# Sliding-window attention and top-1 experts on one core: a chunk's two score halves made next to each other, its second exponentials ahead of the other chunk's transposes' copy, and logits and row sums handled for several chunks at once

## The chip, the cores and the metric

One core of one Trainium2 chip runs the whole program in one launch. The metric is the device time of one execution in microseconds (us); the time before is the median of three runs, 646.98 us (646.08 to 647.4).

## The reference, cut to what matters

```
B, H, S, D = 8, 8, 576, 64            # attention
scores = q @ k.T / sqrt(D) + slope[h] * -(i - j)   where 0 <= i - j < 128, else -1e9
p = exp(scores - rowmax);  attn = p / (p.sum(-1) + 1e-9);  x = attn @ v    -> (4608, 512)
E, F = 8, 1024                        # experts, one for each token
logits = x @ w_gate;  e = argmax(logits);  gate = softmax(logits)[e]
out = gate * (relu(x @ w1[e]) @ w2[e])
```

Everything is float32. The expert part first needs to know which tokens go to which expert, and so the whole attention.

## The kernel before, in words

The 4608 tokens are worked on in 36 **chunks** of 128 query rows. Nine chunks make up two sequences: four of the first sequence (block m = 0, 1, 2, 3), one **tail chunk** with the last 64 rows of both, four of the second sequence. For m = 0 there is only one block of keys, otherwise two. A chunk passes through these stages; the line numbers are those of the profile of before.

- **Score half** `g` = 0 or 1 (four heads each; `scores`, L167 and L176): TensorE writes the bias (bfloat16 products with `eye_sb`) and then the products of `q_sb` and `k_sb` into one of two PSUM tiles, `s0` and `s1`, which take turns. All of these matmuls use 64 x 64 quarters of the array, four at a time. The first half of a chunk is in `s0`, the second in `s1`.
- **Weigh** (`weigh`): VectorE folds the band with a predicated copy (L189, not for m = 0) and takes the row maximum `nmax` (L192); ScalarE makes four exponentials (L198) into `pe`, each followed by a read of its accumulator, the row sum `rsum`. These free the score tile.
- **Transposes** of a half (`transposes`, L211): four 128 x 128 transposes on TensorE into a bank of PSUM (`b_ps`, two buffers), ScalarE copies it to `pT` (L213), GpSimd masks it with two selects (L221, L223).
- **Value products** (`av`, L239): `pT` times `v_sb`, 128 x 64 of the array, into another `b_ps`. They are short for a chunk with m = 0. ScalarE copies the result to `xT` (L286).
- **Rows** (`rows`): VectorE takes the reciprocal of `rsum` (L246); TensorE multiplies `xT` with the identity and the gate weights (L249, "logit products" below) into the single tile `r_ps`; VectorE scales both parts (L254) into `x_sb`, sums the logits over heads (`done`, L1220), and SyncE's queue writes the rows to `xd` in DRAM (L1227). GpSimd adds 1e-9 to `rsum` (`guard`, L182).

The order on every engine is written by hand: time is cut into **steps**, four for each chunk, and `LAGS` says at which step after 4 x chunk each stage k stands: 0 and 4 are the score halves, 2 and 5 their maxima and exponentials, 1 and 6 the transposes, 7 and 8 the value products, 3 the rows, 9 the copy to `xT`; `rank` sorts within a step. So TensorE always has stages of several chunks in a row: scores of chunk c beside transposes of c-1, value products of c-2 and logit products of c-3 or c-4. Every engine runs its list in order and waits on semaphores.

After a group of 3 to 6 chunks (`GROUPS`) `route` ranks the group's tokens by expert, in five stages spread over steps, most of them at every fourth step: mostly small VectorE operations, two bursts of small matmuls (L490 to L494, and L537). Steps also carry DMA loads (`load_q`, `load_v`, `load_k`, expert weights `w_raw`), GpSimd's scaling of `q_sb` (L70), and from step `FETCH` on the rounding of the first expert weights, half a matrix at a time, on ScalarE (L1011) and GpSimd (L1016).

Around step 144 the first expert's early tokens are gathered (`e_xg`); they go through TensorE transposes (L672, at two steps, "p0" and "p1"), a ScalarE cast `e_xh` (L674) and the first layer (L711) between the last chunks. From about 217 us TensorE does the layers of the experts (L711, L907) to the end.

Of the kernel before, what the change touches and what calls it, by code (L numbers as in the profile page):

```python
# [21 lines left out]
QB = 32  # L22
# [13 lines left out]
def attention(ctx, tc, st, qT, kT, v, iw, load_c2, chunk_done, chunks, begun):  # L36
# [75 lines left out]
    eps_sb = const.tile([128, H], F32, name="eps_sb")  # L112
# [68 lines left out]
    def guard(rsum):  # L181
        nc.gpsimd.tensor_tensor(out=rsum, in0=rsum, in1=eps_sb, op=ALU.add)  # L182

    def weigh(g, pe, rsum, s_ps, m, tail, lo, hi, later=False, add=True):
# [9 lines left out]
        def exps(pairs=range(2)):  # L194
            for n in pairs:
# [6 lines left out]
            if add and g and 1 in pairs:  # L202
                guard(rsum)
# [39 lines left out]

    def rows(ch, subs, xT, rsum):
        rinv = small.tile([128, H], F32, name="rinv")
        nc.vector.reciprocal(out=rinv, in_=rsum)  # L246
# [3 lines left out]
        x_sb = xp.tile([128, NP, XW], F32, name="x_sb")  # L250
        for lo, n in ((128, E), (0, D)):
            cols = slice(lo, lo + 2 * n)
            split = lambda ap: ap[:, :, cols].rearrange("q p (c x) -> q p c x", c=2)
            nc.vector.tensor_tensor(  # L254
                out=split(x_sb), in0=split(r_ps),
# [19 lines left out]
    for ch in range(len(chunks)):  # L275
# [4 lines left out]
        if ch in SPLIT:  # L280
            plan.setdefault(4 * ch + 3, []).append((10, ch))
# [6 lines left out]
    def do(k, ch):  # L288
        if k == 9:
            return copy_x(ch)  # L290
        if k > 10:
            h = slice(4 * k - 44, 4 * k - 40)
            nc.vector.tensor_reduce(out=sums[ch][:, h], in_=pes[ch][:, h, :], axis=AX.X, op=ALU.add)
            return guard(sums[ch]) if k == 12 else None
        if k == 10:
            exps = second.pop(ch)
            exps((0,))
            copy_x(ch - 2)
            return exps((1,))
        subs = chunks[ch]  # L300
        if k in (0, 4):
            if k == 0:
                pes[ch] = pp.tile([128, H, 128], F32, name="pe")
                sums[ch] = small.tile([128, H], F32, name="rsum", bufs=8)
            live[ch] = scores(subs, k // 4)
        elif k in (2, 5):
            second[ch] = weigh(k // 3, pes[ch], sums[ch], *live.pop(ch), later=k == 5 and ch in SPLIT, add=ch not in SUMS)
# [3 lines left out]
        elif k == 3:  # L311
            rows(ch, subs, xTs.pop(ch), sums.pop(ch))
# [981 lines left out]
```

## Time and profile before

| what | value |
|---|---|
| median of 3 runs | 646.98 us (646.08 to 647.4) |
| profiled execution, its own time | 646.91 us |
| span from its first to its last instruction | 645.2 us |
| TensorE (PE) matmul busy | 632.1 us, 98% |
| VectorE (DVE), ScalarE (ACT), GpSimd (POOL) busy | 390.9, 314.1, 299.2 us |
| granted TensorE clock, mean | 0.998 |

The profile gives each instruction's engine, line, output and inputs, start and duration; times are from the span's start. "Idle" notes in brackets name what ended a wait. Matmuls are pipelined: one that is listed with 0.32 us is followed by the next after much less, so the price of a stage is read from start to start. ScalarE's and VectorE's operations overlap their neighbours a little in the same way. PEld is TensorE's loading of weights.

### The profile page before, as it was taken

What the parts mean: (1) busy time and instruction counts of PE and PEld (TensorE: products, weight loads), DVE (VectorE), ACT (ScalarE), POOL (GpSimd) and SP (SyncE); (2) the same over time, 40 slices, a digit from 0 to 9 for tenths busy, and PEclk for the clock granted to TensorE, in tenths of its full rate; (3) what the DMA queues carried; (4) which work ended last, traced back from release to release, by engine and by line L of the source; (5) the groups of instructions that cost most, each with busy time, mean ns of one, the idle gap of its engine ahead of it and who ended that gap; (6) DMA issues with size and microseconds to landing.
All of it is one profiled execution on the core that took longest, in us unless ns stands there. A gap on an engine that the chain in (4) does not pass through costs nothing.

```text
span 645.2 us, 15063 instructions
## 1 busy us (share of the span) xinstructions
PE 632.1 (98%) x5681; PEld 540.2 (84%) x5681; DVE 390.9 (61%) x978; ACT 314.1 (49%) x947; POOL 299.2 (46%) x414
## 2 busy tenths in 40 slices
PE   8999999999998999999999999999999999999995
PEld 4888888888887988888988898898898888888884
DVE  6578888969898785545544654555455355346411
ACT  5878889888867324433333334334233333424311
POOL 5534657769446040166236707633660660561202
PEclk9999999999999999999999999999999999999999
DMA  9958998988734263372534325333442542534101
GB/s 312 301 153 216 220 260 237 217 258 240 193 69 103 54 196 98 130 273 75 186 128 151 108 78 183 113 94 139 142 122 83 165 122 87 185 107 143 65 0 62
DMA packets 57645, 97.90 MB, mean 152 GB/s; under 512 B 11669, under 2 KB 31765, under 8 KB 56674
## 3 DMA queue, kind: packets, MB, share of 16 engines
q1 hardware_dynamic: 49090, 76.89, 39.9%
q0 software_dynamic: 8336, 19.76, 10.6%
q8 instruction: 46, 0.75, 0.5%
q10 hardware_dynamic: 144, 0.26, 0.2%
q14 instruction: 29, 0.24, 0.1%
HBM read 77.91 MB, written 18.98 MB: 150 GB/s over the span
## 4 chain that ended last, share of the span: by engine, by line
PE 67%; ACT 0%; DVE 0%; issue 0%; POOLq 0%; POOL 0%; ACTq 0%
PE y_ps L907 32%; PE l_ps L711 30%; PE s_ps L711 2%; PE x_ps L672 1%; PE b_ps L239 1%; PE y_ps L867 1%; PE r_ps L249 0%; PE x_ps L867 0%; ACT pe L198 0%; POOLq L1060 0%; PE l_ps L683 0%; DVE y L915 0%; DVE nmax L192 0%; ACT e_xh L674 0%; DVE s_ps L189 0%
## 5 line engine op out<-in xcount | busy, mean ns | idle before, releaser
L714 ACT ACTIVATE hh<-l_ps 128x336 fp32r<-128x336 f32 (+7 forms) x104 | 45.9, 446 | 203.4 <-PE l_ps L711 176.9
L718 DVE SCALAR_TENSOR_TENSOR hl<-l_ps,hh 128x336 fp32r<-128x336 f32 (+7 forms) x104 | 51.7, 501 | 152.4 <-ACT hh L714 137.5
L691 POOL DMA_INDIRECT xg<-xd,od_idx x112 | 114.8, 1025 | 35.1 <-issue 34.8
L198 ACT ACTIVATE pe<-s_ps,nmax 128x128 f32<-128x128 f32 x288 | 102.9, 382 | 33.7 <-DVE nmax L192 27.0
L907 PE MATMUL y_ps<-wh,hh 128*128 128x512 f32 (+5 forms) x280 | 111.0, 397 | 0.0
L907 PE MATMUL y_ps<-wh,hl 128*128 128x512 f32 (+5 forms) x280 | 110.4, 394 | 0.0
L907 PE MATMUL y_ps<-wl,hh 128*128 128x512 f32 (+5 forms) x280 | 110.3, 394 | 0.0
L895 POOL DMA_INDIRECT out<-y,od_pidx x33 | 34.6, 1049 | 147.8 <-ACT y L913 141.2
L999 DVE TENSOR_TENSOR wl<-w_raw,wh 128x512 fp32r<-128x512 f32 x114 | 73.9, 690 | 32.0 <-ACT wh L995 27.4
L711 PE MATMUL l_ps<-xh,wh 128*128 128x304 f32 (+9 forms) x416 | 81.8, 318 | 0.3 <-DVE hl L718 0.3
L711 PE MATMUL l_ps<-xl,wh 128*128 128x304 f32 (+9 forms) x416 | 81.1, 316 | 0.3 <-issue 0.3
L711 PE MATMUL l_ps<-xh,wl 128*128 128x304 f32 (+9 forms) x416 | 81.0, 317 | 0.0
L711 PEld LDWEIGHTS l_ps<-xh,wh 128*128 128x128 f32 x416 | 68.0, 189 | 9.0 <-issue 1.2
L711 PEld LDWEIGHTS l_ps<-xl,wh 128*128 128x128 f32 x416 | 66.3, 189 | 2.3 <-issue 0.6
L711 PEld LDWEIGHTS l_ps<-xh,wl 128*128 128x128 f32 x416 | 66.4, 189 | 1.9
L239 PE MATMUL b_ps<-pT,v_sb 128*64 128x128 f32 (+2 forms) x1136 | 65.4, 265 | 0.4 <-ACT pT L213 0.4
L239 PEld LDWEIGHTS b_ps<-pT,v_sb 128*64 128x64 f32 (+1 forms) x1136 | 56.1, 136 | 10.0 <-issue 4.9
L907 PEld LDWEIGHTS y_ps<-wh,hl 128*128 128x128 f32 (+5 forms) x280 | 51.4, 184 | 13.7 <-DVE hl L718 0.2
L907 PEld LDWEIGHTS y_ps<-wl,hh 128*128 128x128 f32 (+5 forms) x280 | 51.5, 184 | 11.3
L907 PEld LDWEIGHTS y_ps<-wh,hh 128*128 128x128 f32 (+5 forms) x280 | 51.4, 184 | 10.4 <-ACT hh L714 0.5
L995 ACT CAST wh<-w_raw 128x1024 fp32r<-128x1024 f32 x57 | 59.5, 1044 | 1.0 <-DMA w_raw<-w 1.0
L198 ACT ACTIVATION_READ_ACCUMULATOR pe<-s_ps,nmax 128x1 f32 x272 | 59.6, 219 | 0.0
(225 smaller groups left out, 958.2 us busy)
## 6 DMA issues: line engine op xcount, KB each, us to landing
w_raw<-w SPq DMA_DIRECT2D x64, 512.0 KB
q_sb<-qT SPq DMA_DIRECT2D x39, 256.0 KB
xd<-x_sb SPq DMA_DIRECT2D x32, 258.0 KB
v_sb<-v SPq DMA_DIRECT2D x32, 256.0 KB
k_sb<-kT SPq DMA_DIRECT2D x7, 1152.0 KB
w_n<-w SPq DMA_DIRECT2D x4, 1024.0 KB
xg<-xd,od_idx POOLq DMA_INDIRECT x112
xd<-x_sb SPq DMA_DIRECT2D x8, 129.0 KB
```

Of the source, the lines that this page charges most:

```text
L198: nc.scalar.activation(out=pe[:, h, :], in_=s_ps[:, c, n, lo:lo + 128], func=AF.Exp, bias=nmax[:, 2 * c + n:2 * c + n + 1], scale=1.0, **( ...
L239: nc.tensor.matmul(out=x_ps[64 * c:64 * c + 64, p, q], lhsT=blocks["v", b, m - 1 + kb][0:kk, D * h:D * h + D], rhs=pT[0:kk, kb, h, q], sta ...
L672: nc.tensor.transpose(out=x_ps[:, d, :], in_=g[:, SUB * d:SUB * d + 128], identity=st["ident"])
L691: ins = tc.nc.gpsimd.indirect_dma_start(out=g[:, s], out_offset=None, in_=parts, in_offset=bass.IndirectOffsetOnAxis(ap=idx[:, s], axis=0),)
L711: nc.tensor.matmul(out=ps, lhsT=a[:, 128 * d:128 * d + 128], rhs=b[:, d], start=(k == 0), stop=(k == 11))
L714: nc.scalar.activation(out=hh, in_=ps, func=AF.Relu)
L718: nc.vector.scalar_tensor_tensor(out=hl, in0=ps, scalar=0.0, in1=hh.bitcast(F32), op0=ALU.max, op1=ALU.subtract)
L867: nc.tensor.matmul(out=ps[m * g:m * g + n], lhsT=hrs[p][:, f, :], rhs=w2s[p][:, f % 4, w * g:w * g + w], start=f == 0, stop=f == 7)
L895: ins = nc.gpsimd.indirect_dma_start(**kw).ins
L907: nc.tensor.matmul(out=ys[t][0:n], lhsT=a[:, tl], rhs=b[:, 512:1024], start=(f == 0 and k == 0), stop=(f == 7 and k == 2))
L995: keep(tc, nc.scalar.copy(out=wh, in_=raw))
L999: keep(tc, eng.tensor_tensor(out=wl[:, sl], in0=raw[:, sl], in1=wh.bitcast(F32)[:, sl], op=ALU.subtract))
```

## The change

Lines of the changed kernel are given with their own numbers (scores L171 and L180, transposes L210, copy of `pT` L212, exponentials L199, value products L238, logit products L252, scaling L257, sum of logits L1228).

1. `LAGS` is new: both score halves of a chunk stand at step 0 (before 0 and 2); the second half's maximum and exponentials at step 2 (before 2 to 3); the second transposes at 6 (before 8, ahead of the step's other work); the rows at 14 (before 17). In chunks 0 to 2 the halves stay apart, and chunk 3's have a transpose of chunk 2 between them.
2. In `PAIRED` chunks (3 to 35) all four second exponentials run together, and the copy of the transposes of the chunk before stands behind them. Before, the copy to `xT` of an older chunk stood between the second exponentials, two and two; now it stands at the next chunk's step 0, after the value products.
3. The value products of the four tail chunks are in one piece; before, a score half stood between their halves.
4. The logits are scaled into a tile of the group (`lg_all`) and summed over heads once for each group. `x_sb` becomes two fixed tiles of 4 x 129 columns whose last column is zeroed once; the DMA to `xd` now reads 128 runs of 516 elements where it read 512 runs of 129.
5. `rsum` of three chunks lies in one tile: one addition of 1e-9 and one reciprocal for three chunks.
6. `FETCH` is 58 instead of 57.

```diff
-SPLIT = range(3, 36)
+PAIRED = range(3, 36)
-LAGS = {None: (0, 5, 0, 17, 2, 2, 8, 11, 11)}
-LAGS.update({ch: (0, 4, 0, 17, 2, 2, 6, 11, 11) for ch in (1, 2)})
...
+LAGS = {None: (0, 5, 1, 14, 0, 2, 6, 11, 11, 12)}
+LAGS.update({ch: (0, 4, 0, 14, 2, 2, 6, 11, 11, 12) for ch in (1, 2)})
...
     def rows(ch, subs, xT, rsum):
-        rinv = small.tile([128, H], F32, name="rinv")
-        nc.vector.reciprocal(out=rinv, in_=rsum)
+        if ch % 3 == 0:
+            inv["of"] = small.tile([128, 3, H], F32, name="rinv", bufs=2)
+            nc.vector.reciprocal(out=inv["of"], in_=rsum)
+        rinv = inv["of"][:, ch % 3, :]
...
-        for lo, n in ((128, E), (0, D)):
+        for dst, lo, n in ((logits(ch), 128, E), (split(x_sb[:, :, 0:128]), 0, D)):
...
         if k == 10:
-            exps = second.pop(ch)
-            exps((0,))
-            copy_x(ch - 2)
-            return exps((1,))
+            return second.pop(ch)()
...
-            nc.vector.tensor_reduce(out=lg[:, g, :], in_=x_sb[:, :, 128:XW].rearrange("q p (c e) -> q e p c", c=2),
-                                    axis=AX.XY, op=ALU.add)
+            if ch == c0 + G - 1:
+                lg = lgp.tile([128, G, E], F32, name="lg")
+                nc.vector.tensor_reduce(out=lg, in_=lgs["all"].rearrange("q g p c e -> q g e (p c)"), axis=AX.X, op=ALU.add)
...
-                                  in_=x_sb[QB * lo:QB * lo + n, :, 0:SUB])
+                                  in_=x_sb[QB * lo:QB * lo + n])
```

How the order moves, as the built programs list it (a row is an engine's instruction: line, operation, output<-inputs, shape; "x8" is eight of a kind). First TensorE in a chunk with two key blocks, before: from the end of the first score half to the second half's bias.

```order
L167 MATMUL s_ps<-bias_sb,eye_sb 64x2x192
L176 MATMUL s_ps<-k_sb,q_sb 64x192 x8
L211 MATMUL b_ps<-c_sb,pe 128x128 x4
L249 MATMUL r_ps<-iw_sb,xT 128x144 x4
L211 MATMUL b_ps<-c_sb,pe 128x128 x4
L167 LDWEIGHTS eye_sb
```

The same engine and place after, from the products of the first score half on.

```order
L180 MATMUL s_ps<-k_sb,q_sb 64x192 x8
L171 LDWEIGHTS eye_sb
L171 MATMUL s_ps<-bias_sb,eye_sb 64x2x192
...
L180 MATMUL s_ps<-k_sb,q_sb 64x192 x8
L210 MATMUL b_ps<-c_sb,pe 128x128 x4
L252 MATMUL r_ps<-iw_sb,xT 128x144 x4
L210 MATMUL b_ps<-c_sb,pe 128x128 x4
L238 MATMUL b_ps<-pT,v_sb 64x128 x16
```

The second half's bias now follows the first half's products directly, and the value products follow the second transposes, where a score half stood.

ScalarE over one chunk while weights are rounded, before.

```order
L198 ACTIVATE pe,rsum<-s_ps,nmax 128x128 x4
L213 COPY pT<-b_ps 128x512
L1011 CAST wh<-w_raw 128x512
L198 ACTIVATE pe,rsum<-s_ps,nmax 128x128 x2
L286 COPY xT<-b_ps 128x512
L198 ACTIVATE pe,rsum<-s_ps,nmax 128x128 x2
L213 COPY pT<-b_ps 128x512
```

And after.

```order
L291 COPY xT<-b_ps 128x512
L212 COPY pT<-b_ps 128x512
L199 ACTIVATE pe,rsum<-s_ps,nmax 128x128 x8
L212 COPY pT<-b_ps 128x512
L1015 CAST wh<-w_raw 128x512
```

All eight exponentials of a chunk now stand behind the copy of the first transposes of the chunk before.

TensorE around the last value products but one, before: the transposes of gathered tokens "p1" (L672) and what follows.

```order
L211 MATMUL b_ps<-c_sb,pe 128x128 x8
L239 MATMUL b_ps<-pT,v_sb 64x128 x16
L672 MATMUL s_ps<-c_sb,e_xg 128x128 x4
L249 MATMUL r_ps<-iw_sb,xT 128x144 x4
L711 MATMUL s_ps<-e_xh,wh 128x256 x4
```

And after.

```order
L252 MATMUL r_ps<-iw_sb,xT 128x144 x4
L210 MATMUL b_ps<-c_sb,pe 128x128 x4
L238 MATMUL b_ps<-pT,v_sb 64x128 x16
L676 MATMUL s_ps<-c_sb,e_xg 128x128 x4
L715 MATMUL s_ps<-e_xh,wh 128x256 x4
```

The logit products that stood between "p1" and the first layer have moved ahead.

More of the change, by code (lines that the diff above doesn't have):

```diff
@@ L33, in keep, with attention @@
     return ins if HELD[0] else tc.keep_in_program_order(ins)
-def attention(ctx, tc, st, qT, kT, v, iw, load_c2, chunk_done, chunks, begun):
+def attention(ctx, tc, st, qT, kT, v, iw, load_c2, logits, chunk_done, chunks, begun):
     nc = tc.nc
@@ L111, in attention @@
     make_bias()
-    eps_sb = const.tile([128, H], F32, name="eps_sb")
+    eps_sb = const.tile([128, 3, H], F32, name="eps_sb")
     nc.gpsimd.memset(eps_sb, 1.0e-9)
@@ L125, in warm_up @@
             keep(tc, nc.tensor.matmul(out=w_ps, lhsT=warm[:, 0:128], rhs=warm, start=True, stop=True))
+    rows_sb = [const.tile([128, NP, SUB], F32, name=f"x_sb{k}") for k in range(2)]
+    for x_sb in rows_sb:
+        nc.vector.memset(x_sb[:, :, 128:SUB], 0.0)
     def early(op):
@@ L192, in weigh, with exps @@
         nc.vector.tensor_reduce(out=nmax, in_=s4[:, :, lo:lo + 128], axis=AX.X, op=ALU.max, negate=True)
-        def exps(pairs=range(2)):
-            for n in pairs:
+        def exps():
+            for n in range(2):
                 for c in range(2):
@@ L290, in do @@
             return copy_x(ch)
-        if k > 10:
+        if k in (11, 12):
             h = slice(4 * k - 44, 4 * k - 40)
             nc.vector.tensor_reduce(out=sums[ch][:, h], in_=pes[ch][:, h, :], axis=AX.X, op=ALU.add)
-            return guard(sums[ch]) if k == 12 else None
+            return
+        if k == 13:
+            whole = sums["all", ch // 3]
+            return nc.gpsimd.tensor_tensor(out=whole, in0=whole, in1=eps_sb, op=ALU.add)
         if k == 10:
-            exps = second.pop(ch)
-            exps((0,))
-            copy_x(ch - 2)
-            return exps((1,))
+            return second.pop(ch)()
         subs = chunks[ch]
@@ L303, in do @@
                 pes[ch] = pp.tile([128, H, 128], F32, name="pe")
-                sums[ch] = small.tile([128, H], F32, name="rsum", bufs=8)
-            live[ch] = scores(subs, k // 4)
+                if ch % 3 == 0:
+                    sums["all", ch // 3] = small.tile([128, 3, H], F32, name="rsum", bufs=3)
+                sums[ch] = sums["all", ch // 3][:, ch % 3, :]
+            live[ch, k // 4] = scores(subs, k // 4)
         elif k in (2, 5):
-            second[ch] = weigh(k // 3, pes[ch], sums[ch], *live.pop(ch), later=k == 5 and ch in SPLIT, add=ch not in SUMS)
+            second[ch] = weigh(k // 3, pes[ch], sums[ch], *live.pop((ch, k // 3)), later=k == 5 and ch in PAIRED, add=ch not in SUMS)
         elif k == 1:
@@ L311, in do @@
         elif k == 3:
-            rows(ch, subs, xTs.pop(ch), sums.pop(ch))
+            rows(ch, subs, xTs.pop(ch), sums["all", ch // 3])
         elif k == 6:
@@ L319, in do @@
             av(subs, pTs.pop(ch), xps[ch], range(NP // 2, NP))
-            if len(lags(ch)) < 10 and ch + 2 not in SPLIT:
+            if len(lags(ch)) < 10:
                 copy_x(ch)
@@ L325, in rank @@
             return 0.5
-        if k == 6 and s == 4 * ch + 8:
-            return 1
-        if k == 1 and s == 4 * ch + 5:
-            return 3.5
+        if ch in PAIRED and k in (5, 10):
+            return 2.4 if k == 5 else 3.5
         return 4.5 if k == 6 and s == 4 * ch + 6 else k
@@ L388 @@
 WN = 7
-FETCH = 57
+FETCH = 58
 WV = (0, 1)
```

37 lines of the change are left out of this document (18 added, 19 removed).

## The prediction, before the run

> **What bounds the kernel now.** I read the stretches first, then who waited for whom, then TensorE's instructions one after the other. Columns of the stretches: from:to, length, busy time of PE, PEld, DVE, ACT, POOL with counts, granted clock, DMA share, GB/s. Of the waits I show TensorE's two longest (us in total, times, longest).
>
> ```profile
> 24.00:188.00 164.00, 164.00 (x2673) 136.83 (x2677) 133.82 (x345) 137.30 (x578) 102.66 (x168) 1.00 0.80 212
> 188.00:217.00 29.00, 26.98 (x370) 23.43 (x363) 23.87 (x76) 16.47 (x62) 10.94 (x17) 1.00 0.36 86
> 217.00:638.40 421.40, 420.76 (x2376) 366.36 (x2374) 216.77 (x526) 144.32 (x251) 169.64 (x188) 1.00 0.39 123
> ```
> ```profile
> PE s_ps L167 <- ACT pe L198: 1.6, 3, 0.9
> PE b_ps L211 <- ACT pT L213: 1.3, 2, 0.8
> ```
>
> TensorE never idles from 24 to 188 us and loses 0.64 us in the expert part (421.40 less 420.76), at full clock; only where attention ends, 188 to 217, are 2.0 us idle. So a microsecond is gained where TensorE's own list gets shorter or one of its few waits goes, and lost where a new wait holds that list up. Work taken from other engines is worth nothing by itself. What attention gains passes through the expert part, which waits for little else.
>
> **The pair of score halves.** TensorE's list in a chunk with short value products (x16), and in one with full ones:
>
> ```profile
> 63.91 1.09 PE L239 MATMUL b_ps<-pT,v_sb 128*64 128x128 f32 x16
> 64.94 0.36 PE L167 MATMUL s_ps<-bias_sb,eye_sb 64*64 64x384 bf16 x4
> 65.87 0.66 PE L211 MATMUL b_ps<-c_sb,pe 128*128 128x128 f32 x4
> 66.37 1.15 PE L249 MATMUL r_ps<-iw_sb,xT 128*128 128x144 f32 x8
> 67.35 0.60 PE L211 MATMUL b_ps<-c_sb,pe 128*128 128x128 f32 x4
> 67.88 0.36 PE L167 MATMUL s_ps<-bias_sb,eye_sb 64*64 64x384 bf16 x4
> ...
> 74.02 0.36 PE L167 MATMUL s_ps<-bias_sb,eye_sb 64*64 64x384 bf16 x4
> 74.20 0.82 PE L176 MATMUL s_ps<-k_sb,q_sb 64*64 64x192 f32 x16
> 74.95 1.97 PE L239 MATMUL b_ps<-pT,v_sb 128*64 128x128 f32 x32
> 76.85 0.30 PE L167 MATMUL s_ps<-bias_sb,eye_sb 64*64 64x256 bf16 x4
> ```
>
> The same block seen in a window that keeps only its last four products, and the one place before where a second half follows a first directly, at the start:
>
> ```profile
> 74.69 0.33 PE L176 MATMUL s_ps<-k_sb,q_sb 64*64 64x192 f32 x4
> ...
> 4.77 0.33 PE L176 MATMUL s_ps<-k_sb,q_sb 64*64 64x64 f32 x7
> 4.89 0.27 PE L167 MATMUL s_ps<-bias_sb,eye_sb 64*64 64x256 bf16 x2
> ```
>
> Within a half a group of four follows the last in (74.69 - 74.20) / 3 = 0.16 us; the next stage, which uses another cut of the array, follows the last group only after 74.95 - 74.69 = 0.26. A second half's bias pays the 0.16 alone: at the start it followed after 4.89 - 4.77 = 0.12 (its groups are narrower). That is 0.10 a pair, and the bias, 0.18 by itself, is about 0.01 shorter in the stream (an estimate). The other boundaries stay as many and as dear. Chunks 4 to 35 make 32 pairs: 32 x 0.11 = -3.5 us. In the four tail chunks the merged value products gain nothing, since there the score half that stood between them goes elsewhere but its free entry is lost with it: I give 0.1 each back, +0.4.
>
> The bounds of a pair: 0 if the 0.10 is the price of what comes next, 0.13 if all of the bias's 0.18 - 0.16 counts. I take 0.11, nearest to the start's row.
>
> One rule of the Trainium skill speaks against this: TensorE: Matmul & The Clock Gate, section "Step-by-step: what each phase is for", has the drain of a matmul overlap the filling for the next. By it the pair saves nothing and the sum below loses its largest term; the 0.26 beside 0.16 says that here, between cuts of the array, something is not overlapped.
>
> **The new waits.** With both halves together, the second half of chunk c+1 needs tile `s1` free 0.85 us after the first half starts (0.18 + 0.49 + 0.16 + rounding, rows above), so all eight exponentials of chunk c must be through, and they now stand behind the copy of the first transposes. The chain, from rows of before:
>
> ```profile
> 83.27 0.66 PE L211 MATMUL b_ps<-c_sb,pe 128*128 128x128 f32 x4
> 83.96 0.58 ACT L213 COPY pT<-b_ps 128x512 f32<-128x512 f32 x1 [0.46 <-PE b_ps L211]
> ...
> 73.41 0.61 ACT L213 COPY pT<-b_ps 128x512 f32<-128x512 f32 x1
> 73.87 0.41 ACT L198 ACTIVATE pe<-s_ps,nmax 128x128 f32<-128x128 f32 x1
> 74.91 0.42 ACT L198 ACTIVATE pe<-s_ps,nmax 128x128 f32<-128x128 f32 x1
> ...
> 17.43 0.37 ACT L198 ACTIVATE pe<-s_ps,nmax 128x128 f32<-128x128 f32 x1
> 17.95 0.36 PE L167 MATMUL s_ps<-bias_sb,eye_sb 64*64 64x384 bf16 x4 [0.46 <-ACT pe L198]
> ```
>
> From the first transposes: 0.69 to their copy, 0.46 to the first exponential, 1.38 for four (73.87 to 74.91 are three steps of 0.345), 1.04 to the start of the last of the next four, 0.52 from there to TensorE's bias: 4.09 us. TensorE from the same point: transposes 0.50, logit products 0.98, transposes 0.53, value products 1.90 or 1.03, then 0.85: 4.76, or 3.89 with short value products. So a full chunk has 0.67 us to spare and a short one waits 0.20. Behind the waiting bias stand all other stages, and TensorE's list is shifted. Short value products within the paired stretch belong to chunks 5, 9, 14, 18, 23, 27 and 32: 7 x 0.20 = +1.4. The second transposes' copy then starts 3.91 us after the first transposes; a weight rounding and the copy to `xT`, about half a microsecond each like it, end near 5.5. The next logit products stand at 4.76 + 0.91 (the rest of the pair) + 0.50 = 6.2, in a short chunk at 5.5: just in time.
>
> VectorE must deliver the maxima in time. Its worst chunk is the one after a burst of ranking matmuls, when nine small operations wait for TensorE and stand ahead of the fold:
>
> ```profile
> 82.33 0.36 PE L167 MATMUL s_ps<-bias_sb,eye_sb 64*64 64x384 bf16 x4
> 83.95 0.70 DVE L189 COPY_PREDICATED s_ps<-mask_sb,s_ps 128x512 f32<-128x512 uint32 x1
> 84.68 0.69 DVE L192 TENSOR_REDUCE nmax<-s_ps 128x4 f32<-128x512 f32 x1
> ...
> 82.78 0.22 DVE L560 TENSOR_SCALAR gate<-gate 128x5 f32<-128x5 f32 x1
> 196.75 0.58 DVE L560 TENSOR_SCALAR gate<-gate 128x3 f32<-128x3 f32 x1
> ```
>
> The maximum ends 3.04 us after the half began (85.37 - 82.33); the first exponential is due after the pair (0.85 + 0.16 + 0.49 + 0.26 = 1.76), 0.69 and 0.46: at 2.91. So it is 0.1 late six times, which matters only in a short chunk; with an operation stretched as at 196.75 (+0.36) more. Between 0 and 6 x 0.4 I take +0.3, near the lower end, since 82.78 is the more usual row.
>
> **Off the path.** VectorE's and GpSimd's savings:
>
> ```profile
> L1220 DVE TENSOR_REDUCE lg<-x_sb 128x8 f32<-128x64 f32 x36 | 9.4, 260 | 0.0
> L192 DVE TENSOR_REDUCE nmax<-s_ps 128x4 f32<-128x512 f32 x72 | 49.6, 690 | 5.8 <-PE s_ps L176 3.5 <-PE r_ps L547 0.2 <-ACT pe L198 0.2
> ```
>
> 36 sums of 0.26 become 8; one of 5 chunks (320 elements) lies between 64 elements at 0.26 and 512 at 0.69: 0.51. So VectorE loses some 5 us of work, and 24 reciprocals; GpSimd 24 additions. TensorE waits for none of these, and I cost them at nothing; they pay for the lateness just named. If VectorE had not that room, the 0.51 would show in the last group alone (below). The two memsets at the start, the later weight rounding (`FETCH`) and fewer, longer runs to `xd` are hidden too: TensorE's waits name no DMA. SyncE's queue issues the `xd` write a step later in the chunk and with it the loads behind, which have over one chunk's time in hand.
>
> **Where attention ends.**
>
> ```profile
> 202.38 0.66 PE L211 MATMUL b_ps<-c_sb,pe 128*128 128x128 f32 x4 [0.78 <-ACT pT L213]
> 205.40 0.66 PE L211 MATMUL b_ps<-c_sb,pe 128*128 128x128 f32 x4 [0.51 <-ACT pT L213]
> 206.47 1.97 PE L239 MATMUL b_ps<-pT,v_sb 128*64 128x128 f32 x32 [0.41 <-ACT pT L213]
> 208.36 0.66 PE L672 MATMUL s_ps<-c_sb,e_xg 128*128 128x128 f32 x4
> 208.86 1.15 PE L249 MATMUL r_ps<-iw_sb,xT 128*128 128x144 f32 x8
> 209.06 0.59 ACT L674 CAST e_xh<-s_ps 128x512 fp32r<-128x512 f32 x1
> 209.74 0.73 PE L711 MATMUL s_ps<-e_xh,wh 128*128 128x256 f32 x4
> ```
>
> The three waits, 0.78 + 0.51 + 0.41 = 1.7 us, come from the last second half at step 2; it now stands at 0 and they should go. In their place: the first layer needs the cast of "p1" 1.38 us after p1's start (209.74 - 208.36), TensorE is free after 0.50, and no logit products lie between any more: 0.88. The last chunk's first transposes need the bank that the copy behind the exponentials frees: 0.69 + 0.46 + 2.76 + 0.61 = 4.5 us after the transposes before, TensorE comes at 4.4: 0.1 and the maximum's lateness, 0.3. The last group's sum is 0.25 longer ahead of its ranking. Together 1.4: a gain of 0.3.
>
> **Sum.** -3.5 + 0.4 + 1.4 + 0.3 - 0.3 = -1.7 us. The profiled execution took 646.91 us, 0.07 under the median of 646.98, so 645.2.
>
> **The rivals.** 0.2% (1.3 us) is what a measurement can tell from no change; so faster is under 645.7, slower over 648.3.
>
> - The forecast, 644.1 to 646.3: 0.42, of which 0.36 is faster.
> - No give-back: the exponentials are through in time in short chunks too, and where attention ends 0.7 more goes. For it speaks that 0.20 is a small difference of two sums of five rows; against it, each row is steady. -3.5 + 0.4 - 1.0 = -4.1: 642.8. 0.18.
> - The waits eat it: 0.35 in each short chunk, because the rounding of weights and the routing exponentials also stand in ScalarE's list, and nothing gained at the end. ScalarE is busy 137 of 164 us, which speaks for it. -3.1 + 2.5 + 0.4 = -0.2: 646.7. 0.25.
> - Slower: VectorE late. Two stretched operations (2 x 0.36) and a little make the maxima 0.85 late in the 24 chunks that hold a routing stage; 0.18 over the 0.67 to spare: 24 x 0.18 = 4.3, so 649.5. It decides from 0.74 on. Against it: 82.78 beside 196.75, most are not stretched. 0.11. The Trainium skill, SBUF — State Buffer, section "Who interferes with whom", lets VectorE and GpSimd shut each other out of a shared pair of ports for a whole instruction; 0.58 beside 0.22 agrees.
> - Pairs save nothing (the 0.10 is owed to what comes next): +1.4 + 0.3 - 0.3 = 648.3. The rows at 4.77 and 4.89 speak against it. 0.04. This is what the rule on drains named above would make of the time.
>
> Faster 0.54, same 0.31, slower 0.15. The range, 642.8 to 647.6, leaves out the two slower cases and little else.
>
> **What would show it.** Right: in a full chunk 0.16 from the last group of a first half to the second's bias; a wait of the scores for `pe` of about 0.2 in the seven short chunks and none in full ones; a wait of about 0.9 at the first L715; TensorE at its first second-layer product (L911) 1.5 to 2.5 us earlier. Wrong: waits of the scores in full chunks, 0.26 left inside the pair, or waits for `xT` at the logit products.

## The result: 1.25% slower, and the profile after

The changed kernel took 655.27 us (median of 5 runs, 653.92 to 656.48), the kernel before 646.98 us (646.08 to 648.26) on the same chip: 1.0125 times as long [1.0113, 1.0137]. Forecast were 645.2 us and a range of 642.8 to 647.6. The profiled executions took 654.91 and 646.91 us, with spans of 653.2 and 645.2.

The stretches of the changed kernel, in the columns known from before:

```profile
24.00:188.00 164.00, 160.14 (x2597) 137.28 (x2591) 126.19 (x295) 133.59 (x568) 95.76 (x146) 1.00 0.71 215
...
217.00:638.40 421.40, 418.60 (x2385) 364.80 (x2382) 217.99 (x533) 143.67 (x252) 166.86 (x185) 1.00 0.40 125
```

TensorE, which never idled from 24 to 188 us, now idles 3.9 us there, and 2.8 us in the expert part instead of 0.6. Its longest waits, in the form shown before:

```profile
PE s_ps L171 <- ACT pe L199: 3.6, 8, 0.9
PE r_ps L541 <- DVE x_sb L257: 1.7, 2, 1.2
...
PE l_ps L715 <- issue: 1.1, 4, 0.5
PE s_ps L180 <- DMA k_sb<-kT: 1.1, 2, 0.6
PE s_ps L715 <- ACT e_xh L678: 0.7, 1, 0.7
PE x_ps L676 <- DMA xg<-xd,idx: 0.7, 1, 0.7
PE r_ps L494 <- DVE x_sb L257: 0.5, 1, 0.5
PE r_ps L551 <- DVE x_sb L257: 0.5, 1, 0.5
```

Of the 3.6 us for the exponentials, 1.6 lie ahead of 24 us, as in the kernel before. Two kinds have grown from a single wait of 0.3 us each: ranking matmuls waiting for the scaling into `x_sb`, and waits of the first layer where no releaser is shown ("issue"). The wait for gathered tokens (`xg`) is new.

How the loss builds up is read from the start of each chunk's first score half, after less before, worked out from both traces. From chunk 5 on 1.51 us of it is only work done earlier (one set of transposes, 0.53, and the logit products, 0.98, of an older chunk), so the last column is the loss:

```
chunk   start after - before   less 1.51
  4           +1.59                -        (first paired chunk is 3)
  5           +1.86              +0.35
  9           +2.08              +0.57
 15           +1.34              -0.17
 19           +1.34              -0.17
 21           +2.50              +0.99
 22           +3.62              +2.11
 28           +4.81              +3.30
 35           +5.78              +4.27
first L621    +4.81   (228.81 against 224.00)
last L911     +7.27   (645.25 against 637.98)
```

Up to chunk 19 the gain of the pairs just pays for the new waits. From the start of chunk 19 to that of chunk 35 4.4 us are lost, and from the first L621 to the last L911 2.5 more. The last 0.7 us lie behind TensorE's last product; that tail differs between all traces of this case anyway, from 6.6 to 7.9 us.

The pairs themselves did what was forecast. TensorE in the changed kernel, behind a burst of ranking matmuls at 105.96:

```profile
106.38 0.82 PE L180 MATMUL s_ps<-k_sb,q_sb 64*64 64x192 f32 x16
107.03 0.33 PE L171 MATMUL s_ps<-bias_sb,eye_sb 64*64 64x384 bf16 x4
107.19 0.82 PE L180 MATMUL s_ps<-k_sb,q_sb 64*64 64x192 f32 x16
107.94 0.66 PE L210 MATMUL b_ps<-c_sb,pe 128*128 128x128 f32 x4
...
109.95 1.97 PE L238 MATMUL b_ps<-pT,v_sb 128*64 128x128 f32 x32
112.76 0.36 PE L171 MATMUL s_ps<-bias_sb,eye_sb 64*64 64x384 bf16 x4 [0.85 <-ACT pe L199]
```

From products to the second half's bias 107.03 - 106.38 = 0.65, from products to the transposes 107.94 - 107.19 = 0.75: the 0.10 per pair. A whole chunk shows it too: where nothing waits and no ranking or tail chunk is in the way (chunks 5, 7, 10 and 29), the next chunk's start comes 0.12 or 0.13 us sooner than before. The last row is what the gain is spent on.

### The profile page after: what moved, and what is told of

The parts are those of the page before. It is cut to its first block, busy times and chain, and to the rows that moved or that the text cites. A ratio compares the mean times of both kernels' runs of the same rounds, so it can differ in the third digit from the quotient of the medians.

```text
span 653.2 us, 14958 instructions
## 1 busy us (share of the span) xinstructions
PE 632.4 (97%) x5681; PEld 543.3 (83%) x5681; DVE 384.8 (59%) x928; ACT 312.9 (48%) x947; POOL 292.8 (45%) x390
## 4 chain that ended last, share of the span: by engine, by line
PE 74%; issue 9%; DVE 6%; DMA 4%; ACT 3%; POOL 2%; SPq 1%; POOLq 0%; ACTq 0%; DVEq 0%
PE l_ps L715 26%; PE y_ps L911 26%; PE b_ps L238 7%; PE s_ps L180 5%; PE r_ps L252 4%; PE b_ps L210 4%; DMA v_sb<-v 3%; ACT pe L199 2%; PE s_ps L171 2%; DVE s_ps L190 1%; POOL out L899 1%; DMA xd<-x_sb 1%; DVE nmax L193 1%; DVE x_sb L257 1%; POOL xg L695 1%
## 5 line engine op out<-in xcount | busy, mean ns | idle before, releaser
L911 PE MATMUL y_ps<-wh,hh 128*128 128x512 f32 (+5 forms) x280 | 110.9, 396 | 0.0
L911 PE MATMUL y_ps<-wh,hl 128*128 128x512 f32 (+5 forms) x280 | 110.4, 394 | 0.0
L911 PE MATMUL y_ps<-wl,hh 128*128 128x512 f32 (+5 forms) x280 | 110.2, 394 | 0.0
L199 ACT ACTIVATE pe<-s_ps,nmax 128x128 f32<-128x128 f32 x288 | 100.1, 383 | 11.0 <-DVE nmax L193 10.5
L715 PE MATMUL l_ps<-xh,wh 128*128 128x304 f32 (+9 forms) x416 | 81.9, 318 | 0.9 <-issue 0.5
L715 PE MATMUL l_ps<-xh,wl 128*128 128x304 f32 (+9 forms) x416 | 81.2, 317 | 0.3 <-issue 0.3
L715 PE MATMUL l_ps<-xl,wh 128*128 128x304 f32 (+9 forms) x416 | 81.2, 316 | 0.3 <-issue 0.3
L715 PEld LDWEIGHTS l_ps<-xh,wh 128*128 128x128 f32 x416 | 67.9, 188 | 9.9 <-issue 2.0
L220 POOL TENSOR_SCALAR_AFFINE_SELECT pT<-pT 128x512 f32<-128x512 f32 x56 | 36.9, 658 | 72.6 <-ACT pT L212 72.1
L715 PEld LDWEIGHTS l_ps<-xh,wl 128*128 128x128 f32 x416 | 66.3, 189 | 2.5 <-issue 0.5
L715 PEld LDWEIGHTS l_ps<-xl,wh 128*128 128x128 f32 x416 | 66.3, 189 | 2.1 <-issue 0.3
L238 PE MATMUL b_ps<-pT,v_sb 128*64 128x128 f32 (+2 forms) x1136 | 65.0, 265 | 0.2 <-DMA v_sb<-v 0.2
L911 PEld LDWEIGHTS y_ps<-wh,hl 128*128 128x128 f32 (+5 forms) x280 | 51.4, 183 | 13.8 <-DVE hl L722 0.2
L238 PEld LDWEIGHTS b_ps<-pT,v_sb 128*64 128x64 f32 (+1 forms) x1136 | 56.2, 136 | 7.3 <-issue 4.4
L911 PEld LDWEIGHTS y_ps<-wl,hh 128*128 128x128 f32 (+5 forms) x280 | 51.5, 184 | 11.4
L199 ACT ACTIVATION_READ_ACCUMULATOR pe<-s_ps,nmax 128x1 f32 x272 | 60.6, 223 | 0.0
L911 PEld LDWEIGHTS y_ps<-wh,hh 128*128 128x128 f32 (+5 forms) x280 | 51.4, 183 | 10.8 <-ACT hh L718 0.6
```

What stands on the lines that cost most here:

```text
L199: nc.scalar.activation(out=pe[:, h, :], in_=s_ps[:, c, n, lo:lo + 128], func=AF.Exp, bias=nmax[:, 2 * c + n:2 * c + n + 1], scale=1.0, **( ...
L220: nc.gpsimd.affine_select(out=part(cut(0)), in_=part(cut(1)), pattern=pat(-1), base=0, channel_multiplier=1, compare_op=ALU.is_gt, fill=0.0)
L238: nc.tensor.matmul(out=x_ps[64 * c:64 * c + 64, p, q], lhsT=blocks["v", b, m - 1 + kb][0:kk, D * h:D * h + D], rhs=pT[0:kk, kb, h, q], sta ...
L715: nc.tensor.matmul(out=ps, lhsT=a[:, 128 * d:128 * d + 128], rhs=b[:, d], start=(k == 0), stop=(k == 11))
L911: nc.tensor.matmul(out=ys[t][0:n], lhsT=a[:, tl], rhs=b[:, 512:1024], start=(f == 0 and k == 0), stop=(f == 7 and k == 2))
```

## Experiments

Theory A was that the pairs put ScalarE's and VectorE's lists on TensorE's path; its rival B, that the other parts of the change (sums, logits, row tiles) lose the time. Ratios are to the kernel before, run beside each kernel on the same chip, with 95% intervals; losses in us are (ratio - 1) x 647. E13 to E18 ran where the kernel before takes 645.5 to 645.7 us, the others where it takes 646.8 to 647.2.

### Which half of the change (E1, E2)

E1 is the kernel before with parts 4 and 5 of the change, in the old order. E2 is the changed kernel with sums, reciprocals and additions made chunk by chunk again:

```diff
-            if ch == c0 + G - 1:
-                lg = lgp.tile([128, G, E], F32, name="lg")
-                nc.vector.tensor_reduce(out=lg, in_=lgs["all"]...)
+            nc.vector.tensor_reduce(out=lg[:, ch - c0, :], in_=lgs["all"][:, ch - c0]...)
...
+        nc.vector.reciprocal(out=rinv, in_=rsum)
```

> The kernel before with the second half of the change alone: logits summed once per routing group, exponential sums of three chunks in one tile (one reciprocal and one guard for three), the two fixed row tiles; order of the stages, rows 17 steps after the chunk's start and weight rounding as before. Theory A (the pairing is what costs: it puts the exponentials and VectorE on TensorE's path): TensorE waits for nothing from 24 to 188 us, as before, and the time is 645 to 648.5. Theory B (the sums do it: a longer sum ahead of the ranking, larger tiles that come free later): 651 or more, with waits of TensorE for DVE or xd.

> The changed kernel with that half undone: a logit sum, a reciprocal and a guard in each chunk again, everything else (pairs, step of each stage, weight rounding one step later) as changed. Theory A: as slow as the changed kernel or a little slower, 655 to 659, since VectorE has some 5 us more work where it is late. Theory B: near the kernel before, 644 to 648.

E1: 648.62 us, 1.0029 [1.0019, 1.0039], +1.9, just above what theory A gave; TensorE idles 0.2 us from 24 to 188 us, chunk 35 starts 0.41 later than before, and the loss is in the expert part. E2: 656.01, 1.0139 [1.0122, 1.0156]. So most of the loss comes with the order, and something with the tiles costs too. E2 still has the row tiles, so it leaves B's share open; that the grouped sums help or hurt can't be told (the intervals of E2 and of the change meet).

### What makes the exponentials late (E3, E5, E6)

The wait of 0.85 at 112.76 is led back through VectorE. Its rows there, and GpSimd's, in the changed kernel:

```profile
106.64 0.63 DVE L564 TENSOR_SCALAR gate<-gate 128x5 f32<-128x5 f32 x1
...
107.88 0.18 DVE L508 TENSOR_REDUCE rank<-pick 128x5 f32<-128x40 f32 x1
108.10 1.11 DVE L510 TENSOR_SCALAR t<-rank 128x5 f32<-128x5 f32 x1
109.25 0.55 DVE L511 TENSOR_SCALAR t<-t 128x5 f32<-128x5 f32 x1
109.70 0.69 DVE L190 COPY_PREDICATED s_ps<-mask_sb,s_ps 128x512 f32<-128x512 uint32 x1
```
```profile
106.60 0.64 POOL L220 TENSOR_SCALAR_AFFINE_SELECT pT<-pT 128x512 f32<-128x512 f32 x1
...
107.91 1.27 POOL L1020 TENSOR_TENSOR wl<-w_raw,wh 128x512 fp32r<-128x512 f32 x1
109.15 0.62 POOL L70 TENSOR_SCALAR q_sb<-q_sb 128x512 f32<-128x512 f32 x1
```

Three scalings of five columns take 0.63, 1.11 and 0.55 us; each ends within 0.03 us of a GpSimd instruction that began before it, while a reduction between them stays at 0.18. The fold of this chunk starts at 109.70, some 1.8 us late. The Trainium skill, SBUF — State Buffer, section "Who interferes with whom", says that VectorE's scalings may take a pair of ports that GpSimd uses as well, held for a whole instruction, and its reductions never; these rows agree.

E3 starts the rounding of weights, whose GpSimd part is the 1.27 us instruction, 32 steps earlier (`FETCH` 26); E5 moves the gate and two scalings to the next routing stage; E6 starts the rounding two steps later (`FETCH` 60):

```diff
-FETCH = 58
+FETCH = 26        (E3)     FETCH = 60        (E6)
...
-    put_gates(tc, st, gate, groups)                      (E5: from the second routing stage ...)
     yield
+    put_gates(tc, st, gate, groups)                      (... to the third, with the two steps of t)
```

> The changed kernel with the weight rounding 32 steps earlier (FETCH 26 for 58, the same step within a chunk): 14 chunks from about 45 us to 115 us hold ScalarE's roundings and GpSimd's subtractions, in place of those from about 94 to 165. If these hold TensorE up (theory A's first cause: a GpSimd subtraction beside VectorE's small operations, and one more copy in ScalarE's list), TensorE's lost time moves with them: over 2.5 us in 24 to 94 where it was about 1, under 2 in 120 to 170 where it was about 3; total 652 to 656. If the ranking of routing groups alone does it, the waits stay at the same places and the total too.

> The changed kernel with four of VectorE's nine small operations taken out of the burst that follows the ranking matmuls and put one chunk later, into the stage after it (gate + 1e-9, its reciprocal, and the two steps of t = round(rank/128)); three of them are those that took 0.64, 1.11 and 0.55 us at 106 us in place of 0.17. Theory A (VectorE's maxima come late after a burst, because small operations run as long as the GpSimd instruction beside them): the 0.92 + 0.56 us that TensorE loses after the burst at 106 us fall under 0.5, and the whole is 651.5 to 654. Rival (it is ScalarE's list that is too full in the second half, whatever VectorE does): the waits for pe stay, 654.5 to 656.5.

> The changed kernel with each weight rounding two steps later within the chunk (FETCH 60 for 58): ScalarE rounds after the copy to xT, where it waits for the next first transposes, and not ahead of that copy; GpSimd's subtraction then starts with the scores, beside the burst. If ScalarE's order is what counts in the 14 chunks with a rounding: the logit products' 0.10 and 0.32 us behind xT go, 653 to 654.5. If GpSimd's subtraction beside VectorE's small operations counts: as slow or slower, 655 to 657.

E3: 655.85, 1.0146 [1.0129, 1.0163]: no gain. Against the changed kernel it lost about 1 us from chunk 5 to chunk 20, where the rounding now ran, and regained 1.2 up to chunk 35; the burst at 106 us still had rounding beside it, so the run did not isolate it. E5: 656.84, 1.0149 [1.0132, 1.0166], a miss that taught something: the loss behind the burst went (chunk 21 started 0.3 earlier than before, not 2.5 later; 0.9 of that is a better start), but the moved operations came back in front of the next stage's matmuls as `PE r_ps L541 <- DVE x_sb L257: 3.1, 2, 2.1`, and that wait slowed TensorE itself (last section).

E6: 651.85, 1.0082 [1.0065, 1.0099], 2.8 us less than the change and more than either expectation gave. ScalarE from one copy of second transposes to the next exponentials, first in the changed kernel, then in E6:

```profile
148.39 0.63 ACT L212 COPY pT<-b_ps 128x512 f32<-128x512 f32 x1
148.85 0.68 ACT L1015 CAST wh<-w_raw 128x512 fp32r<-128x512 f32 x1
149.37 0.65 ACT L291 COPY xT<-b_ps 128x512 f32<-128x512 f32 x1
...
151.66 0.37 ACT L199 ACTIVATE pe<-s_ps,nmax 128x128 f32<-128x128 f32 x1 [0.80 <-DVE nmax L193]
```
```profile
146.22 0.63 ACT L212 COPY pT<-b_ps 128x512 f32<-128x512 f32 x1
146.69 0.65 ACT L291 COPY xT<-b_ps 128x512 f32<-128x512 f32 x1
147.16 0.69 ACT L1015 CAST wh<-w_raw 128x512 fp32r<-128x512 f32 x1
...
148.59 0.37 ACT L199 ACTIVATE pe<-s_ps,nmax 128x128 f32<-128x128 f32 x1
```

The rounding goes behind the copy to `xT`, which TensorE's logit products wait for, and the next exponentials find their maxima ready instead of 0.80 us late. GpSimd's share of the rounding, which can lock VectorE out, moves with it: in E6 the three scalings of the burst shown above take 1.95 us together instead of 2.29, and from chunk 19's start to chunk 20's E6 loses 0.4 us less than the change. Otherwise the two effects were not taken apart.

### The ranking matmuls (E4, E10, E11)

In the changed kernel the second stage of the group that starts with chunk 21 looks like this on TensorE:

```profile
179.67 0.60 PE L210 MATMUL b_ps<-c_sb,pe 128*128 128x128 f32 x4
180.75 0.18 PE L494 MATMUL r_ps<-oh,tri 128*128 128x48 bf16 x1 [0.48 <-DVE x_sb L257]
```

The ranking writes into a spare corner of `r_ps`, the tile that the scaling of the chunk's rows is still reading. A hand-written table, `PACE`, gives this group's stages their steps. In the old order the rows stood at steps 4c + 17, one step ahead of its entries 122, 126 and 130; the change moved the rows to 4c + 14, into the same steps, and left the table. E10 moves the entries, E11 has that and E6's `FETCH`, E4 gives the ranking a bank of its own:

```diff
-PACE = {21: (122, 126, 130, 132, 135), ...
+PACE = {21: (119, 123, 127, 131, 135), ...          (E10; E11 with FETCH = 60)
-FREE_T = 146
+FREE_T = 0                                          (E4)
```

> The changed kernel with the ranking matmuls' results in a bank of the ring (FREE_T 0 for 146) and no longer in the free columns of the logit tile, which the row scaling must have read first. Theory A: the 2.7 us that TensorE waits there for x_sb (L541, L494, L551) go, less what the ring's extra turn costs (a first transpose that waits for the copy to xT, up to 0.3 us for each of 12 bursts): 652 to 655. Rival: these waits only stand in for the exponentials, which TensorE would have waited for right after; then 655 as before.

> The changed kernel with one row of the table that sets the steps of the routing of chunks 21 to 26 moved: (119, 123, 127, 131, 135) for (122, 126, 130, 132, 135), so that no stage falls into the step of the row scaling or ahead of the fold. Theory: the change moved the rows three steps earlier within the chunk's rhythm and left this table; the waits of L494 at 179.7 (0.5), L551 at 185.6 (0.5) and L541 at 192.4 us (1.2) for x_sb then go: 653.0, between 652.3 and 653.8. Rival: VectorE is behind there in any case and another wait takes their place: 654.5 to 656.

> The changed kernel with that row of the table and with the weight rounding two steps later (651.85 alone): if both act apart from each other, 649.7 (649 to 650.4).

E4, a miss: 662.75, 1.0240 [1.0223, 1.0257]. Outside `r_ps` the ranking takes one of the two `b_ps` banks and waits for ScalarE's copies, which now stand behind eight exponentials:

```profile
PE b_ps L541 <- ACT pT L212: 6.4, 5, 1.7
PE b_ps L494 <- ACT pT L212: 3.4, 4, 1.6
```

E10: 653.13, 1.0091 [1.0074, 1.0107], 2.2 us less; of the waits for `x_sb` those of L494 and L551 are gone from its list, and of L541's 1.7 us one wait of 0.5 remains.

E11: 650.43, 1.0047 [1.0030, 1.0064], 5.1 us less than the change, against 2.8 + 2.2 = 5.0 for its parts: as far as intervals of more than 1 us either way can tell, the two are separate losses.

### The row tiles and a load that came 210 us later (E7, E8, E9, E12, E15 to E18)

E7 is the kernel before with nothing but the fixed row tiles (and whole rows written to `xd`). E8 adds an idle GpSimd instruction to each chunk of the kernel before, E9 both, since the waits for "issue" had raised the question whether the place of instructions in the program matters. E12 is E11 with row tiles of 144 columns instead of 129, written in 516-byte runs:

```diff
+    rows_sb = [const.tile([128, NP, SUB], F32, name=f"x_sb{k}") for k in range(2)]     (E7, E9)
...
+        if s % 4 == 3 and s < 144:
+            nc.gpsimd.memset(pad, 0.0)                                                 (E8, E9)
...
+    rows_sb = [const.tile([128, NP, XW], F32, name=f"x_sb{k}") for k in range(2)]      (E12)
```

> The kernel before with the row tiles of the change alone: two fixed tiles of 4 x 129 columns, written to xd whole, the logits in a tile of their own, still summed in each chunk. All the changed kernels lose 0.9 to 1.1 us more than the kernel before at one place of the expert part (a group of first-layer products at 282 to 290 us, in front of which nothing shown is missing) and 0.3 to 1.0 at another (463 to 472). If the tiles or the shape of the rows in xd do it: 648.0 to 648.8, with both. If not: 646.5 to 647.3.

> The kernel before with one idle GpSimd memset of one column in each chunk, 36 in all, which only makes the program longer. If the lost time of the expert part hangs on where the code lies: that place changes (0.3 to 1.1 us either way) and the time with it, 646.2 to 648.5. If not: the same waits at the same places and 646.8 within 0.5.

> The kernel before with the row tiles of the change (649.4 by themselves, 2.3 us slower, all of it in the expert part) and the 36 idle GpSimd memsets, which alone took away 0.5 us of the wait at 282 us and left the time as it was. If the loss of the row tiles is a matter of where the code comes to lie: under 1.2 us of wait at that place in place of 1.9, and 647 to 648.3. If it is what the rows do (their shape in the DMA, the tiles): 649 to 650.

> The kernel of the run before this one with row tiles 144 columns wide, of which 129 are written to xd as before the change (runs of 516 bytes in place of 2064). If the shape of the rows in the DMA makes the loss in the expert part (1.9 us with the new row tiles by themselves): 647.8 (647.2 to 648.4). If the tiles or the code do: 649.7 as the run before it.

E7: 649.43, 1.0037 [1.0022, 1.0051], with nothing lost before 217 us. E8: 647.71, 1.0007 [0.9997, 1.0017]. E9, between its two expectations: 648.91, 1.0028 [1.0018, 1.0037]. E12, a miss: 657.15, 1.0161 [1.0140, 1.0182], with one wait of 3.0 us at L621. Padding is neutral alone and no cure; that the narrow tiles made it worse is not explained.

A further part came from the SyncE queue. One load of 1 MB, `w_n`, is issued before almost everything else in the kernel before, and at the end of attention in the changed one. The queue of each (SPq is SyncE's DMA queue):

```profile
10.96 0.38 SPq L856 DMA_DIRECT2D w_n<-w  x1
```
```profile
221.11 0.38 SPq L860 DMA_DIRECT2D w_n<-w  x1
...
222.99 1.00 SPq L569 DMA_DIRECT2D xd<-gate  x2
```

The cause is where its tile lies. The two row tiles and `lg_all` push the pools of attention up in SBUF; in the built programs `w_n`'s tile begins at byte 219,456 of a partition, the last pool of attention ended at 217,472 before and ends at 220,192 after. Where they overlap, the load must wait until attention has done with that pool. E15 to E18 test this on the kernel before: two row tiles allocated and zeroed on VectorE but never used (E15), fixed row tiles of 144 columns that are used (E16), two tiny tiles zeroed on VectorE (E17), and two row tiles of which GpSimd clears one column (E18, 4 KB of each partition and no work in the loop):

```diff
+    rows_sb = [const.tile([128, NP, SUB], F32, name=f"x_sb{k}") for k in range(2)]
+    for x_sb in rows_sb:
+        nc.gpsimd.memset(x_sb[:, 0, 0:1], 0.0)          (E18; E15: nc.vector, [:, :, 128:SUB])
```

> The kernel before with the two row tiles of the change made and cleared and then not used. If their place in SBUF, or the two memsets, make the loss in the expert part: 649 to 650. If not: 647.2 within 0.5, and the wait at 282 us 0.9 as before.

> The kernel before with its 144-column row tiles fixed (two, used in turn) and not from a pool; logits, sums and rows to xd as before. If fixed tiles make the loss in the expert part (a pool's tile is released, these never are): 649 to 650. If the logits' own tile or the whole rows do: 647.2 within 0.5.

> The kernel before with two more VectorE memsets at the start, of 4 columns each (16 bytes of SBUF in place of the row tiles' 4 KB). If the two instructions make the loss that the unused row tiles bring (3.1 us): 2 to 3.5 us slower. If not: within 0.5 of the kernel before.

> The kernel before with the two row tiles in SBUF, unused, and one column of each cleared on GpSimd, so that VectorE's list is as before. If the 4 KB that all later tiles are moved by make the loss: 2 to 3.5 us slower. If VectorE's memsets do: within 0.5 of the kernel before.

E15: 648.83, 1.0054 [1.0037, 1.0071]. E16: 645.96, 1.0005 [0.9996, 1.0015]. E17: 645.92, 1.0006 [0.9996, 1.0016]. E18: 648.47, 1.0049 [1.0032, 1.0065]. In E15 and E18, where attention's pools end at byte 221,632, `w_n` is issued after 222 us; in E16 and E17, where they end at 217,472 and 217,536, near 11. So 4 KB of room cost 3.2 us [2.1, 4.2]. SyncE's queue, and GpSimd's first gather of the expert part, in E17 and then in E18:

```profile
219.59 3.33 SPq L569 DMA_DIRECT2D xd<-gate  x5
```
```profile
226.31 1.24 POOL L667 DMA_INDIRECT xg<-xd,idx  x1 [16.27 <-DVE idx L624]
```
```profile
219.26 2.19 SPq L569 DMA_DIRECT2D xd<-gate  x4
222.45 0.39 SPq L860 DMA_DIRECT2D w_n<-w  x1
222.89 0.50 SPq L569 DMA_DIRECT2D xd<-gate  x1
```
```profile
228.78 0.97 POOL L667 DMA_INDIRECT xg<-xd,idx  x1 [18.84 <-DVE i_n L889]
```

The last gates are written behind `w_n`, the gather comes 2.5 us later, and TensorE, which does not wait for it in E17, does in E18: `PE x_ps L676 <- DMA xg<-xd,idx: 2.8, 2, 1.7`. That the place costs this is shown; that it is the gate behind `w_n` that holds up the gather is read from the order alone.

### What is left (E13, E14)

E13 is E11 with the old row tiles and logits in the pool, so that `w_n` is early again; the sums of three chunks stay. E14 is E13 with the second half of six chunks one step later, behind the transposes: four with short value products ahead of them (8, 21, 26, 30) and two with full ones (20, 33):

```diff
-        for dst, lo, n in ((logits(ch), 128, E), (split(x_sb[:, :, 0:128]), 0, D)):
+        x_sb = xp.tile([128, NP, XW], F32, name="x_sb")                                (E13)
...
+LAGS.update({ch: (0, 5, 1, 14, 1, 2, 6, 11, 11, 12) for ch in (8, 20, 21, 26, 30, 33)})   (E14)
```

> The changed kernel with later rounding and the moved table row (650.4) and, beyond that, rows and logits in one 144-column tile of a pool with a logit sum in each chunk, as before the change; what is left of the change are the pairs and the sums of three chunks. If the row tiles cost their 2.3 us here too, less 0.7 for the chunk sums: 648.8 (648.0 to 649.5). If they are only slow in the old order: 650.4 to 651.2.

> The run before this one with six of the pairs taken apart again: in chunks 8, 20, 21, 26, 30 and 33 the second half stands behind the first transposes, 0.5 us later. TensorE waits there for the second exponentials of the chunk before, 0.35, 0.56, 0.32, 0.41, 0.33 and 0.56 us in the run with both moves. Theory (a pair pays only where the exponentials are through): 2.5 us less waiting, 0.1 to 0.15 more for each, so 1.6 to 1.9 faster: 647.0 (646.2 to 647.8). If the exponentials only fall further behind (the next chunk waits): no change, 648.5 to 649.5.

E13: 646.71, 1.0017 [1.0007, 1.0026], the best version and still not faster than before: +1.1 us, which on the scale of 647 is 648.1, as expected if the row tiles cost. TensorE's longest waits are now for the exponentials and for loads of `v_sb`:

```profile
PE s_ps L167 <- ACT pe L195: 3.4, 9, 0.9
PE b_ps L234 <- DMA v_sb<-v: 1.5, 2, 1.0
```

E14: 650.05, 1.0067 [1.0050, 1.0083], a miss. The wait for the exponentials fell to 1.8, but the transposes now waited, for the bank that ScalarE's copy frees behind the same exponentials: `PE b_ps L206 <- ACT pT L208: 4.1, 6, 0.9`. Five of these six waits, 3.7 us, are in chunks that were taken apart (all but 21); the sixth, 0.43 us at 209 us, E13 has too. So it is ScalarE's chain, not TensorE's order, that sets the pace of these chunks.

## Why the prediction was wrong

**The pairs (-3.5).** Right: the rows at 106.38 to 107.94 give 0.10, and undisturbed chunks come 0.12 or 0.13 us sooner. The rival that pairs save nothing falls, and with it what the prediction made of the rule on drains here.

**Short chunks (+1.4).** The sum came out nearly right, but size and count were both wrong. The first short chunk that waits, TensorE and ScalarE of the changed kernel:

```profile
41.56 0.66 PE L210 MATMUL b_ps<-c_sb,pe 128*128 128x128 f32 x4
...
44.78 0.82 PE L180 MATMUL s_ps<-k_sb,q_sb 64*64 64x192 f32 x16
45.77 0.36 PE L171 MATMUL s_ps<-bias_sb,eye_sb 64*64 64x384 bf16 x4 [0.17 <-ACT pe L199]
```
```profile
42.81 0.37 ACT L199 ACTIVATE pe<-s_ps,nmax 128x128 f32<-128x128 f32 x1
...
45.22 0.41 ACT L199 ACTIVATE pe<-s_ps,nmax 128x128 f32<-128x128 f32 x1
```

The bias comes 45.77 - 44.78 = 0.99 after the products instead of 0.65: 0.34 lost, though the wait is listed with 0.17. Two more such chunks (26 and 30) lose 0.40 and 0.32 with 0.23 and 0.15 listed, so what a wait costs is read from the starts. The chain was 4.21 us long (45.77 - 41.56) where five rows gave 4.09: 0.10 of it ahead of the first exponential, 0.03 at its end. Two sums differing by 0.20 can't carry a term that is multiplied by 7.

Where a short chunk waits in full, it loses 0.32 to 0.40, as the rival "the waits eat it" had it. But it does so in three of seven places. Chunks 12 and 17 lose nothing to the exponentials: ranking matmuls of about 0.36 us stand there between the value products and the pair, and the working had left them out. Chunks 21 and 35 lose 0.16 and 0.09, the latter behind shorter ranking matmuls. That makes 1.3 us in the changed kernel and, read in the same way, 1.5 in E11. That two errors balanced is luck.

**VectorE late (+0.3).** The step that failed is "82.78 is the more usual row", and with it "which matters only in a short chunk": at one burst three scalings were locked out at once and cost TensorE 0.92 + 0.56 = 1.5 us in a full chunk (20), reckoned from the starts at 112.76 and 114.16. Waits of the scores in full chunks were the sign of being wrong that the prediction had named. The same burst at 78.3 us met a chunk without a fold and cost nothing. So not 24 late chunks, as the rival on the slow side had it, but one that lost more than a us. Once the table row is moved, chunk 33, a full one too, is late behind a routing stage as well: in E13 chunks 20 and 33 lose 0.46 + 0.55 and 0.80 + 0.55 us, 2.4 together, by the starts of their score halves.

**Costed at nothing.** The main failure. "TensorE waits for none of these" was true of the old order, in which ScalarE had room. ScalarE's exponentials and copies, 24 to 188 us, with what they waited for, before and after:

```profile
L198 ACT ACTIVATE pe<-s_ps,nmax 128x128 f32<-128x128 f32 x236 | 85.5, 383 | 24.4 <-DVE nmax L192 18.3 <-DVE c L524 2.0 <-DVE p L515 1.6
...
L213 ACT COPY pT<-b_ps 128x512 f32<-128x512 f32 x58 | 35.4, 611 | 1.4 <-PE b_ps L211 1.4
```
```profile
L199 ACT ACTIVATE pe<-s_ps,nmax 128x128 f32<-128x128 f32 x232 | 81.6, 384 | 4.0 <-DVE nmax L193 3.9
...
L212 ACT COPY pT<-b_ps 128x512 f32<-128x512 f32 x57 | 34.6, 607 | 26.5 <-PE b_ps L210 24.7 <-POOL pT L222 1.8
```

ScalarE idles about as long as before (30.4 us of the 164 instead of 26.7), but ahead of the copy, where it waits for TensorE, and no longer ahead of the exponentials, where the idle time was slack. So what stands in its list between copies counts: the place of the rounding, on ScalarE and GpSimd together, cost 2.8 us (E6). The forecast had seen this spot ("just in time") and given it no term. The routing table was not weighed against the move of the rows at all: 2.2 us (E10), by waits that the working did not consider, since it counted only what TensorE's list loses and what ScalarE delays. And the row tiles were costed as two memsets; their place in SBUF moved a load. That could have been read in advance, in the order of SyncE's queue: in the traces it is the queue's 15th transfer before and its 156th after.

**The end of attention (-0.3).** The wait at the first L715 came as forecast (0.7 for 0.88). From chunk 35 (+4.27) to the first L621 (+4.81) 0.5 was lost instead of 0.3 gained, and 1.0 more by the first tokens' transposes, where `xg` was late. In E13, without the row tiles and with a sum in each chunk, the same stretch is 0.3 shorter than before, as forecast; which of the two did it was not tested.

**The sum.** The change lost 8.1 us [7.3, 8.9]. The rounding's place is 2.8 of it and the table 2.2, together 5.1 (E11). From E11 to E13, each by its own ratio, 1.9 goes with the row tiles and `w_n`, with E18's 3.2 beside it for the place alone. The 1.1 of E13 is what the forecast of -1.7 should have hit. E13's trace is best laid beside E17's, the kernel before with two tiny tiles, whose runs took much the same time as those of the kernel before beside them. Chunk 35 starts 1.4 us later in E13 (the 1.51 taken off), the first L621 product 0.9 later, and from there to the last product both take 412.6 us. So the end gains 0.5, and what failed is attention, for which -3.5 + 0.4 + 1.4 + 0.3 = -1.4 was forecast. With 1.5 for the short chunks, 2.4 for VectorE late and the 1.5 us that E13 waits for `v_sb` and the kernel before does not, it comes to +2.3. That is no full account of the 1.4, and this execution (647.80) is one of E13's slower ones. But VectorE late is the term of the sum that was most too small.

**Open.** Among E1 to E12 all kernels with row tiles show 0.7 to 1.2 us of waits named "issue" in one group of first-layer products (285 to 301 us), where the kernel before shows 0.3. So does E7, where `w_n` is early; the ScalarE activation ahead of that group starts after 6.0 us of idle time there, 3.8 in the kernel before, and the trace names nothing in the program that ends it. None of E13 to E18 has these waits, and E17 takes 412.6 us from the first L621 product to the last product where the kernel before takes 414.0 in its own, earlier trace. So something besides the kernels differs between the two sets of runs. E7's 2.4 us are not settled, and neither is how much of the 1.9 between E11, whose trace has 0.7 us of these waits, and E13 belongs to the row tiles. The 0.5 us at the start (`k_sb`) differ from run to run.

## What to carry to other kernels

When stages move in a hand-made order, move with them every table that was tuned to their place, and read the instruction order of the DMA queues too: a load that changes rows says that its memory is now shared with something that finishes late. An engine's share of idle time says nothing of slack; ask in front of which instruction it idles, and after the change ask again. A term that is a small difference of two long chains, times many, needs a range as wide as its neighbours' spread, since one late row among five decides its sign, and a count that looks at each of the places: here three of seven had other work in between.

## What the runs showed of the hardware that was not expected

A wait of 2 us can halve TensorE's clock. E5 in two stretches (columns: length, PE busy, granted clock, DMA share, GB/s), and the rows behind the wait:

```profile
194.00:202.00 8.00, 6.06 (x62) 0.57 0.41 109
202.00:210.00 8.00, 8.00 (x118) 1.00 0.42 111
```
```profile
195.94 0.64 PE L541 MATMUL r_ps<-rr,lp 128*128 128x48 bf16 x12 [2.06 <-DVE x_sb L257]
...
196.83 1.49 PE L180 MATMUL s_ps<-k_sb,q_sb 64*64 64x192 f32 x16
```

The clock falls to 0.57 in the stretch with the wait, and sixteen products take 1.49 us instead of 0.82. The Trainium skill, TensorE: Matmul & The Clock Gate, section "Part 1: The HAM clock gate (the "warmup" mystery)", ties the slow clock to an idle window of about 3.4 us; here a wait of 2.06 us was enough, and the measurement decides. The clock fell too at a wait of 3.0 us in E12 (0.66 from 230 to 234 us) and at one of 1.7 in E4 (0.83 from 200 to 210 us). But two waits of 1.7 us, in E15 and E18, left it at 1.00 from 226 to 238 us, and so did waits of up to 1.2 in the changed kernel (1.00 from 24 to 217 us). So the length of a single wait does not decide it alone, and no run here shows what else does.
